# Linear attention and spectral mixing on one core: sixteen rows of one weight transfer cut into short and long transfers

## The chip, the core and the metric

The kernel runs on one core of one Trainium2 chip. A core has a matrix engine (TensorE, PE in the profile, with its weight loads listed as PEld), a vector engine (DVE), a scalar engine (ACT), a general engine (GpSimd, POOL) and a queue processor (SyncE, SP), and 16 DMA engines that move data between the chip's main memory (HBM) and the on-chip memory (SBUF, 128 partitions). POOL and SP issue the transfers; the DMA engines carry them out.

The metric is the device time of one execution in microseconds (us), as the median of three runs: 421.13 us before the change (421.12 to 421.89).

## What is computed

The reference, cut to what matters here:

```python
def _attn_ref(q, k, v):                      # (8 batches, 8 heads, 576, 64)
    q_p, k_p = phi(q), phi(k)                # elu + 1
    kv  = einsum('bhsd,bhse->bhde', k_p, v)
    num = einsum('bhsd,bhde->bhse', q_p, kv)
    den = einsum('bhsd,bhd->bhs', q_p, k_p.sum(axis=2))[..., None] + 1e-06
    return num / den                         # x: (8, 576, 512) after the heads are joined

def _moe_ref(x, w_r, w_i, w_ch):             # w_r, w_i: (64 modes, 512, 512) f32
    X = rfft(x, axis=1)
    Xr, Xi = real(X[:, :64]), imag(X[:, :64])
    Yr = einsum('bmd,mde->bme', Xr, w_r) - einsum('bmd,mde->bme', Xi, w_i)
    Yi = einsum('bmd,mde->bme', Xr, w_i) + einsum('bmd,mde->bme', Xi, w_r)
    u = x + irfft(Y, n=576, axis=1)          # Y: Yr + iYi in the first 64 modes, else 0
    return u + maximum(u @ w_ch, 0.0)
```

Nearly all the data is in `w_r` and `w_i`: 64 modes x 512 x 512 float32 each, 134 MB together. Each of these numbers is used once per execution, with 8 batches.

## The kernel before, in words

The kernel has three stages. In the first, q, k and v of the 8 batches are loaded, the attention is computed and its result is transformed to the 64 modes. In the last, the result is transformed back, added, multiplied by `w_ch` and stored. Between them, and the longest, is the stage of the modes. It takes the 64 modes in 32 pairs, `mode_pair(p)` for p from 0 to 30 and `last_pair()` for p = 31 (called `LAST`).

**What one pair needs.** Pair p needs the two matrices of modes 2p and 2p+1 from `w_r` and the two from `w_i`. `w_load(p, half, ...)` issues one transfer from POOL for `half` 0 (`w_r`) and one for `half` 1 (`w_i`). One transfer reads 64 rows of 8192 consecutive float32 numbers each and writes them, turned into bfloat16, to every second of the 128 partitions of the tile `w{p}` (`w_in[p][half::2]`, 16 blocks of 512 numbers per partition). That is 2 MB read and 1 MB written per transfer, 16 KB written per row.

**What uses it.** `mode_pair(p)` runs 16 products (`product`, line 432 of the profile) of that tile with the transformed input, into one accumulator `P`. The first of them waits until both transfers of the pair have landed. Then `evacuate` (lines 447 and 449) copies `P` out and `picks` (line 455) sorts the rows. `work_slot` fits pieces of the other stages in between (for instance lines 726, 736, 745, 751 and 752), and `keep_warm` (line 419) runs matmuls whose result is not used.

**What sets the order.** The order on every engine is written out by hand: `pin` keeps instructions in the order of the program. The pairs 5 to 31 share two buffers (`W_KEEP = 2`). So the transfers of pair p+2 are issued by POOL after the 16 products of pair p have read the buffer; POOL issues the `w_r` half, then the `w_i` half, and waits for the next buffer. Two pairs are therefore in flight or in use at any time. POOL does nothing else in this stage. Each transfer raises one of eight completion counters, taken in turn; an issue that takes a counter again waits for the counter's previous transfer.

**The last pair.** `w_load_last` (line 129) splits the last pair: `w_r` and `w_i` of mode 62, `w_r` of mode 63, and `w_i` of mode 63 in five pieces (`PIECES`: 2, 2, 2, 1 and 1 of 8 blocks). `last_pair` uses each piece as soon as it has landed (`y_last`, line 513). After the last piece the rest hangs on its result: line 519, lines 932 to 945, the exchange of rows in `YZ_all` (line 947), and the final sums and stores (lines 760 to 834).

Of the kernel before, what the change touches and what calls it, by code (L numbers as in the profile page):

```python
# [43 lines left out]
def kernel(  # L44
# [10 lines left out]
    nc = tc.nc  # L55
# [7 lines left out]
    NDW = 4 * NDC  # L63
    NDL = NDW // 2
# [41 lines left out]
    pin = tc.keep_in_program_order  # L106
    PIECES = (slice(0, 2), slice(2, 4), slice(4, 6), slice(6, 7), slice(7, 8))
    HALVES = [slice(0, 64), slice(64, 128)]

    LAST = NM // 2 - 1  # L110

    def w_load(p: int, half: int, pool, tag: str, bufs: int):
        if half == 0:
            w_in[p] = pool.tile([128, NDW, D], BF16, tag=tag, bufs=bufs, name=f"w{p}")
        two = (moe_w_r, moe_w_i)[half][2 * p : 2 * p + 2]
        pin(
            nc.gpsimd.dma_start(  # L117
                out=w_in[p][half::2], in_=two.rearrange("g (r dc) e -> (g r) dc e", dc=NDW)
            )
        )  # L120

    def w_load_last(pool, tag: str, bufs: int):
        w_in[LAST] = pool.tile([128, NDW, D], BF16, tag=tag, bufs=bufs, name=f"w{LAST}")
        for g in range(2):
            for half in range(2):
                rows_in = (moe_w_r, moe_w_i)[half][NM - 2 + g].rearrange("(p dc) e -> p dc e", dc=NDL)
                for dcs in PIECES if (g, half) == (1, 1) else (slice(0, NDL),):
                    dst = w_in[LAST][half::2, g * NDL + dcs.start : g * NDL + dcs.stop]
                    pin(nc.gpsimd.dma_start(out=dst, in_=rows_in[:, dcs, :]))
# [16 lines left out]
    def w_next():  # L146
        p, half = pending.pop(0)
        pool, tag, bufs = (wpool, "w", W_KEEP) if p < n_keep else (wpre, "wp", W_PRE)
        w_load(p, half, pool, tag, bufs)
# [258 lines left out]
    def w_get(p: int):  # L408
        if p not in w_in and p == LAST:
            w_load_last(wpool, "w", W_KEEP)  # L410
        elif p not in w_in:
            for half in range(2):
                w_load(p, half, wpool, "w", W_KEEP)
        return w_in[p]
# [14 lines left out]
    def product(P, x, n: int, w, dc: int, n_dc: int):  # L429
        c = dc % NDC * 32  # L430
        pin(
            nc.tensor.matmul(  # L432
                P[c : c + n, :], x, w[:, dc, :],
                start=(dc < NDC), stop=(dc >= n_dc - NDC), tile_position=(0, c),
                skip_group_check=True,
            )
        )

    def set_diagonal(p: int):
        for h in range(2):  # L440
            src = xt_v[HALVES[h], :, :, :, p].rearrange("p c t b -> p c (t b)")
            pin(nc.vector.tensor_copy(out=xz[p % 2][HALVES[h], :, h, :], in_=src))  # L442
# [19 lines left out]
    def mode_pair(p: int):  # L462
# [5 lines left out]
        for dc in range(NDW):  # L468
            product(P, xz[p % 2][:, dc].rearrange("p h n -> p (h n)"), 32, w, dc, NDW)
        if p + 1 < LAST:  # L470
            set_diagonal(p + 1)
# [15 lines left out]
    def last_pair():  # L487
        xl = ystage.tile([128, NDL, 2 * B], BF16, name="xl")
        for h in range(2):
            src = xt_v[:, (2 * h + 1) * NDC : (2 * h + 2) * NDC, :, :, LAST]  # L490
            pin(
# [3 lines left out]
            )  # L495
        w = w_get(LAST)
        kk = NM - 2
# [91 lines left out]
    def x_of(t: int):  # L589
        if t < B * NJJ:  # L590
            return x_main[t // NJJ][:, t % NJJ, :]
        i = t - B * NJJ
        return x_tail[i // 2][:, i % 2, :]
# [352 lines left out]
    for h, eng in enumerate((nc.sync, nc.gpsimd)):  # L946
        eng.dma_start(
            out=YZ_all[64 * h : 64 * h + 64 : NF // NL].rearrange("r b z d -> r b (z d)"),
            in_=last.rearrange("p z d -> p (z d)"),
# [15 lines left out]
    def sums_of(n: int, i: int):  # L965
# [8 lines left out]
            out=x_of(0), in0=accs[0][:, 0], scalar=0.0, in1=x_of(0), op0=ALU.max, op1=ALU.add  # L974
# [50 lines left out]
```

## Time and profile before

| | |
|---|---|
| Median of three runs | 421.13 us (421.12 to 421.89) |
| Span of the profiled execution, first to last instruction | 419.4 us |
| Median less span, what lies around the instructions | 1.7 us |
| TensorE busy | 317.2 us (76% of the span) |
| VectorE / ScalarE / GpSimd busy | 231.3 / 154.2 / 57.4 us |
| DMA engines, packets of POOL's transfers | 93.4% of the time of all 16 engines |
| One weight transfer (62 of them), median from issue to landing | 13.2 us (`w_r`), 17.5 us (`w_i`) |
| POOL's issue of one weight transfer, median | 0.544 us |
| Mean granted TensorE clock | 0.83 of full speed |

How to read it: the profile is of one execution. An engine is busy while one of its instructions runs; the DMA share is the time that packets took on the 16 DMA engines. "Issue to landing" of a transfer counts its waiting behind earlier transfers in the same queue. The trace also holds every packet of the DMA engines, with its queue, start, duration and size, and for each transfer 16 completion marks, one from each DMA engine. It doesn't say which engine a packet or mark belongs to; but each engine's packets follow each other at a fixed step, so that its packets can be followed by their times. Queue q0 holds the transfers that POOL issues, q1 those of SP; q8 and q14 are the engines' own reading of their programs.

### The profile page before, as it was taken

The page shows a single profiled execution, that of the slowest core. Times are in us where ns is not written, and L with a number is a line of the kernel's source. Part 1 is how long each engine was busy: PE and PEld are TensorE (multiplying, and loading weights), DVE is VectorE, ACT ScalarE, POOL GpSimd, SP SyncE. Part 2 cuts the span into 40 slices and gives each one's busy share as a digit, 9 for nine tenths or more (in the row PEclk, how much of TensorE's full clock was granted, in tenths as well). Part 3 has the DMA queues.
Part 4 walks back from the last instruction along what each step waited for, and adds up shares of the span by engine and source line. Part 5 has one row for each costly group of instructions (what it writes and reads, how often), then busy time and mean ns, then how long its engine had stood idle before and what let it go on. Part 6 is the DMA issues. An engine that isn't in the chain of part 4 may idle for free.

```text
span 419.4 us, 7466 instructions
## 1 busy us (share of the span) xinstructions
PE 317.2 (76%) x3143; PEld 164.4 (39%) x3143; DVE 231.3 (55%) x509; ACT 154.2 (37%) x253; POOL 57.4 (14%) x100
## 2 busy tenths in 40 slices
PE   0369998999617875676767686988798877998993
PEld 0257776877301332222222233433343332453421
DVE  4588899785314563463645353464456443522794
ACT  4677798854201011000000233334253432330783
POOL 4222224210011211111111111111111111130000
PEclk9999999579855658665655599899899997899998
DMA  8999999999999999999999999999999999998698
GB/s 217 211 212 216 210 222 203 228 206 223 217 223 208 218 220 209 220 217 212 220 214 213 223 213 214 223 210 216 220 209 219 217 214 219 216 209 166 235 391 328
DMA packets 17073, 93.17 MB, mean 222 GB/s; under 512 B 2112, under 2 KB 3024, under 8 KB 12880
## 3 DMA queue, kind: packets, MB, share of 16 engines
q0 software_dynamic: 12496, 81.48, 93.4%
q1 hardware_dynamic: 4544, 11.22, 7.2%
q8 instruction: 24, 0.39, 0.3%
q14 instruction: 9, 0.07, 0.0%
HBM read 163.93 MB, written 9.44 MB: 413 GB/s over the span
## 4 chain that ended last, share of the span: by engine, by line
DMA 64%; PE 23%; DVE 4%; POOL 3%; ACT 3%; issue 2%; DVEq 0%; ACTq 0%; POOLq 0%
DMA w<-in_moe_w_i_dram 53%; DMA pick_sb<-row_pick 8%; PE P L432 6%; DMA k<-in_k_dram 3%; PE acc L760 3%; PE kvp L257 3%; PE acc L800 2%; POOL w L117 2%; PE z L726 1%; DVE x L293 1%; ACT ke L208 1%; PE xf L355 1%; PE zl L419 1%; PE qTp L237 1%; PE num L163 1%
## 5 line engine op out<-in xcount | busy, mean ns | idle before, releaser
L432 PE MATMUL P<-w,xz 128*32 128x512 bf16 x496 | 42.6, 475 | 37.6 <-DMA w<-in_moe_w_i_dram 35.4
L419 PE MATMUL zl<-wch,id 128*128 128x512 f16 x185 | 58.2, 466 | 0.0
L449 ACT CAST ys<-P 128x512 f16<-128x512 f32 x15 | 8.8, 586 | 132.4 <-PE P L432 132.4
L117 POOL DMA_DIRECT2D w<-in_moe_w_r_dram x31 | 17.3, 559 | 246.4 <-PE P L432 211.8
L447 DVE CAST ys<-P 128x512 f16<-128x512 f32 x17 | 11.8, 692 | 51.0 <-PE P L432 51.0
L706 PE MATMUL eps<-wch,xTw 128*128 128x512 f16 x144 | 39.3, 399 | 0.0
L432 PEld LDWEIGHTS <-xz 128*32 128x32 bf16 x496 | 12.6, 108 | 63.3 <-DMA w<-in_moe_w_i_dram 40.3
L163 PEld LDWEIGHTS <-qT 64*128 64x128 f16 (+1 forms) x640 | 22.6, 122 | 29.6 <-issue 15.6
L689 ACT CAST x16w<-x_main 128x512 f16<-128x512 f32 x32 | 19.8, 618 | 37.8 <-DVE x_main L687 37.8
L687 DVE TENSOR_TENSOR x_main<-ya,x_main 128x512 f32<-128x512 f32 x32 | 22.0, 689 | 16.5 <-PE ya L683 16.3
L257 PE MATMUL kvp<-vpad,ke 32*128 32x130 f16 x576 | 24.3, 263 | 8.9 <-ACT qT L244 6.1
L442 DVE COPY xz<-xt_c 64x256 bf16<-64x256 bf16 x62 | 23.0, 371 | 10.9 <-PE P L432 10.0
L419 PEld LDWEIGHTS <-id 128*128 128x128 f16 x185 | 18.9, 112 | 25.6 <-issue 14.3
L714 ACT CAST E<-eps 128x512 f16<-128x512 f32 (+1 forms) x40 | 21.2, 540 | 17.7 <-PE eps L706 17.7
L257 PEld LDWEIGHTS <-ke 32*128 32x128 f16 x576 | 22.3, 116 | 10.6 <-issue 8.6
L163 PE MATMUL nw<-kv_sb,qT 64*128 64x65 f16 (+1 forms) x320 | 18.2, 231 | 9.8 <-DVE x_tail L650 4.7
L237 PE MATMUL qTp<-id,qe 128*128 128x128 f16 x144 | 15.1, 289 | 10.6 <-DVE qe L221 9.5
L293 DVE TENSOR_TENSOR x<-num,rd 128x512 f16<-128x512 f32 x32 | 22.1, 692 | 1.1
L650 DVE TENSOR_TENSOR x_main<-nw,rd 128x256 f32<-128x256 f32 x32 | 11.2, 416 | 18.8 <-PE nw L163 18.8
L455 PE MATMUL yt<-pick_sb,ys 128*128 128x32 f16 (+1 forms) x128 | 8.8, 185 | 16.7 <-DMA pick_sb<-row_pick 9.4
L698 DVE COPY xTw<-xTp 128x512 f16<-128x512 f16 x36 | 15.0, 416 | 10.3 <-PE xTp L696 10.3
L208 ACT ACTIVATE qe<-q 128x1152 f16<-128x1152 f16 (+1 forms) x16 | 17.9, 1157 | 7.2 <-DMA q<-in_q_dram 7.1
(118 smaller groups left out, 507.5 us busy)
## 6 DMA issues: line engine op xcount, KB each, us to landing
w<-in_moe_w_r_dram POOLq DMA_DIRECT2D x31, 1024.0 KB, 13.2
w<-in_moe_w_i_dram POOLq DMA_DIRECT2D x31, 1024.0 KB, 17.5
out_dram<-x_main SPq DMA_DIRECT2D x12, 512.0 KB, 3.6
k<-in_k_dram POOLq DMA_DIRECT2D x8, 576.0 KB, 12.9
v<-in_v_dram POOLq DMA_DIRECT2D x8, 576.0 KB, 14.3
q<-in_q_dram POOLq DMA_DIRECT2D x7, 576.0 KB, 12.6
out_dram<-x_main SPq DMA_DIRECT2D x8, 256.0 KB, 4.0
q<-in_q_dram SPq DMA_DIRECT2D x2, 576.0 KB, 4.5
```

The source lines that it names most:

```text
L117: nc.gpsimd.dma_start(out=w_in[p][half::2], in_=two.rearrange("g (r dc) e -> (g r) dc e", dc=NDW))
L163: mm = nc.tensor.matmul(num[hpo][orow, c0 : c0 + 65], qT[rows, hpp, h2, cols], kv_sb[rows, hpp, h2, :])
L208: pin(nc.scalar.activation(out=ev[:, c], in_=heads(nm, b, c), func=AF.Exp))
L257: nc.tensor.matmul(kv_ps[:, h2, 0:130], phi["k", b][r0 : r0 + 32, j // NJ, j % NJ].rearrange("p o d -> p (o d)"), vp[r0 : r0 + 32, :, j, 0 ...
L293: nc.vector.tensor_tensor(out=dst.rearrange("p (o c d) -> p o c d", o=2, c=4), in0=nv[:, :, :, 0:64], in1=rden.unsqueeze(3).broadcast_to([ ...
L419: pin(nc.tensor.matmul(last_ps[0], id16, wch16[:, 0, :]))
L432: nc.tensor.matmul(P[c : c + n, :], x, w[:, dc, :], start=(dc < NDC), stop=(dc >= n_dc - NDC), tile_position=(0, c), skip_group_check=True,)
L442: pin(nc.vector.tensor_copy(out=xz[p % 2][HALVES[h], :, h, :], in_=src))
L687: pin(nc.vector.tensor_tensor(out=x, in0=acc, in1=x, op=ALU.add))
L689: pin(nc.scalar.copy(out=x16w[t], in_=x))
L706: nc.tensor.matmul(e_ps, xT[:, c, :], wch16[:, c, :], start=(c == 0), stop=(c == NDC - 1))
L714: pin(nc.scalar.copy(out=dst, in_=e_ps[:, cols]))
```

## The change

The `w_r` transfer of pair 21 (modes 42 and 43) is issued as five transfers in place of one. Rows 0 to 47 go as one transfer of 48 rows. Rows 48 to 55 go as two transfers of 8 rows: each row's 16 blocks of 512 numbers are seen as two halves of 8 blocks; the short transfer takes the first block of each half (two runs of 512 numbers per row), the long one the other seven of each half (two runs of 3584 numbers per row). Rows 56 to 63 go the same way. The same bytes land in the same places. All other transfers are as before.

```diff
+    CUT = (21, 0)
 
     def w_load(p: int, half: int, pool, tag: str, bufs: int):
         if half == 0:
             w_in[p] = pool.tile([128, NDW, D], BF16, tag=tag, bufs=bufs, name=f"w{p}")
         two = (moe_w_r, moe_w_i)[half][2 * p : 2 * p + 2]
-        pin(
-            nc.gpsimd.dma_start(
-                out=w_in[p][half::2], in_=two.rearrange("g (r dc) e -> (g r) dc e", dc=NDW)
-            )
-        )
+        rows_in = two.rearrange("g (r dc) e -> (g r) dc e", dc=NDW)
+        if (p, half) != CUT:
+            pin(nc.gpsimd.dma_start(out=w_in[p][half::2], in_=rows_in))
+            return
+        dst = w_in[p].rearrange("p (h d) e -> p h d e", h=2)
+        src = rows_in.rearrange("p (h d) e -> p h d e", h=2)
+        pin(nc.gpsimd.dma_start(out=w_in[p][half : 2 * 48 : 2], in_=rows_in[0:48]))
+        for lo in (48, 56):
+            for d0, d1 in ((0, 1), (1, NDL)):
+                pin(
+                    nc.gpsimd.dma_start(
+                        out=dst[half + 2 * lo : 2 * lo + 16 : 2, :, d0:d1, :],
+                        in_=src[lo : lo + 8, :, d0:d1, :],
+                    )
+                )
```

Here `NDW` is 16, `NDL` is 8 and `D` is 512. In the changed program POOL issues 106 instructions instead of 102, in the same order otherwise. The first products of pair 21 wait for the five transfers of `w_r` and the one of `w_i`, and the issue for pair 23, which takes the buffer again, names these six. The later transfers keep their places relative to each other in the turn of the eight counters.

## The prediction

> **What bounds the kernel now.** I read the page's span, slices and queues first. The third number in a queue's row is the share of the 16 DMA engines' time over the span.
>
> ```profile
> span 419.4 us, 7466 instructions
> ...
> DMA  8999999999999999999999999999999999998698
> ...
> q0 software_dynamic: 12496, 81.48, 93.4%
> q1 hardware_dynamic: 4544, 11.22, 7.2%
> q8 instruction: 24, 0.39, 0.3%
> q14 instruction: 9, 0.07, 0.0%
> ```
>
> The DMA engines are full from the first slice to slice 37 (about 388 us). TensorE is busy too, but much of that is filler, so I read next the chain of work that ended last, around pair 21 and at the end of the loads (start, length, what):
>
> ```profile
> 253.72 17.46 DMA w<-in_moe_w_i_dram
> 271.18 0.04 issue
> 271.22 1.07 PE P L432 x16
> 272.29 0.29 issue
> 272.58 0.54 POOL w L117
> 273.12 17.50 DMA w<-in_moe_w_i_dram
> 290.62 0.04 issue
> ...
> 369.52 1.01 PE P L432 x16
> 370.52 0.29 issue
> 370.81 2.16 POOL w L129 x4
> 372.98 13.65 DMA w<-in_moe_w_i_dram
> 386.63 0.05 issue
> 386.67 0.36 PE y_last L513 x8
> ```
>
> A pair's products start 0.04 us after its `w_i` half has landed, and `y_last` 0.05 us after a piece of the last pair. So the end follows the last landings. The issue at 272.58 is pair 21's. Its long wait is not a gap: the queue still holds pair 20. Landings of whole transfers follow each other every 4.85 us from 130 to 375 us, whatever the issues do. What sets the time is the DMA engine that finishes last.
>
> That is the third view, the DMA share in 40 slices from 380 to 388 us (0.2 us each):
>
> ```profile
> DMA  9599599569889989999899334666566555454100
> ```
>
> It falls from 9 to 3 at 384.4 us and ends only at 387.6. So the 16 engines do not finish together. Following their packets (each 16 KB packet takes 1227 ns and the next starts 1208 ns after it) I find the ends: six engines at 384.20 to 384.42, one at 384.73, two at 386.45 and 386.60, seven at 387.34 to 387.62. At 23 us all 16 landing marks of a transfer lay within 0.34 us.
>
> The cause is in q8 and q14, the reading of programs. A q8 packet is 16 KB, and 23 of the 24 come before 388 us. Their durations repeat in a cycle of eight (975, 975, 962, 893, 893, 948, 945, 935 ns): eight engines take turns. From 140 us on, the engine hit loses 858 to 940 ns. That makes three hits for seven engines and two for the eighth (hit at 219.0, end at 386.60). The q14 packets (8 KB, 322 ns) hit two others in turn, 300 ns each time. These end at 384.73 and 386.45. Thus eight **program-reading engines** are late (seven of them by 3 us), and of the other eight one is late by 2.1 us.
>
> **The change, part by part.** All is worked against the profiled execution: 419.4 us of span, 1.7 us less than the median of 421.13.
>
> *Rows 0 to 47.* 48 rows over 16 engines are 3 packets instead of 4: each engine saves 1208 ns.
>
> *Four transfers of 8 rows.* Each has 16 packets: 1 KB written in the short, 7 KB in the long. Rows of q0: 1 KB takes 98 ns, 2 KB 173, 8 KB 625, 16 KB 1227; less the overlap of 19 ns the steps are 79, 154, 606 and 1208 ns. A 7 KB packet lies between 2 and 8 KB; on their line it is 531 ns. Completion marks add about 21 ns per transfer and engine (a weight transfer takes 4853 ns, four steps are 4832): 84 ns for four.
>
> The trace of before has no transfer of 8 rows, so which engines take these packets is open. Per engine, against the 4853 ns before:
> - the short ones on eight engines, two packets each: -1208 + 4 x 79 + 84 = **-0.81 us** for those;
> - the long ones on the other eight: -1208 + 4 x 531 + 84 = **+1.00 us** for those;
> - both kinds on the same eight: -1208 + 4 x 610 + 84 = +1.32 us there, -1.12 on the others;
> - spread evenly over 16: -1208 + 2 x 610 + 84 = +0.10 us everywhere.
>
> Below nothing the bound is -1.12 us, above it +1.32. I take short and long on opposite eights, since the two kinds are separate transfers that each fill eight engines with two packets.
>
> The Trainium skill speaks to this on the page "DMA: Bandwidth & Descriptors", section "Why a DMA increments its semaphore by 16 and not by 1": a software-issued transfer over fewer than 16 engines goes to consecutive engines from a cursor that goes round. By that rule the short ones meet on one eight and the long ones on the other; no run here shows it yet.
>
> *What counts of this.* The delay of an engine stays with it to the end, since its queue never runs dry: the fetch delays above did. So the landing that ends the loads moves by the sum on the latest engine. There are two answers for opposite eights. If any of the seven latest engines gets long packets, the end moves from 387.62 to between 387.34 + 1.00 = 388.34 and 388.62: **+0.7 to +1.0 us**. If all eight program-reading engines get the short ones, they end at 386.8, but the engine at 386.45 goes to 387.45, which is then last: 387.45 - 387.62 = **-0.2 us**.
>
> *Issue on POOL.* Four more issues at 0.544 us (rows of L117) are 2.18 us: the `w_i` half of pair 21 is issued from 275.30 instead of 273.12. Nothing else queues behind it on POOL until 282.34. The earliest engine needs it only at 282.43, the first landing mark of pair 21's `w_r`; the exchange near the end, into an idle queue, took 2.0 us from POOL's issue (390.49) to its first packet (392.47). Issued by 275.85, it is ready at 277.8, with 4.6 us of cover (3.8 on an engine that saves 0.81 us). Price nothing; without the cover it would be at most 2.18 us. The first short pieces are covered as well: the first issue still ends at 273.12, and pair 20 keeps even the earliest engine until 277.58.
>
> *Waits.* The products of pair 21 wait for six transfers instead of two; the `w_i` half lands last by 4.85 us, so the five others are done. The issue for pair 23 names six transfers that have landed before the products it also waits for. SP has no transfers of its own in this stretch. Nothing.
>
> *Cost per transfer.* The pieces of the last pair measure it: 128 KB pieces land 0.63 to 0.64 us apart, 64 KB ones 0.32 to 0.34, against 0.61 and 0.30 for their share of a whole transfer: 0.02 to 0.04 us each, packets included. This is in the sums. The page named above, section "Anatomy of one DMA", gives about 2.0 us fixed per such transfer. By it four more in line would cost 8 us and end at 429 us; the rows above say that the queue hides that part.
>
> *After the loads.* If the landings come 1.0 us later, pair 29's `w_i` lands at 369.3, still before its products at 369.52; pair 30's products (378.10, on a landing at 378.05) and `y_last` follow the landing. POOL's last issue at 378.34 moves to 379.3 and is ready at 381.3, before the earliest engine comes to it (384.2, or 383.4 with short packets). All later work hangs on line 519 and shifts whole.
>
> Sum for the likeliest case: at least one of the seven latest engines in the long eight, likely one of the last ones: +0.7 to +1.0, I take +0.97. Span 420.4, median **422.1 us**.
>
> **The rivals.**
> *A, no slower: the short packets fall on exactly the eight program-reading engines.* -0.2 us, 420.95 us. For it: these eight are a closed group, and the two q14 engines lie outside it, as if engines were given out in halves. Against it: nothing shows that the group is a run of eight, or that the short transfers start on it. The point of decision: all seven of the latest engines must be spared; one in the long eight is enough for +0.7. Even then the gain cannot reach 0.2%: the engine at 386.45 takes back 0.63 of the 0.81 us.
> *B, all four on the same eight engines.* +1.32 (422.45 us) if one of the seven is there; otherwise the engine at 386.45 ends at 387.77, +0.15 (421.3 us). For it: 8 rows may be handed out from the same first engine each time. Against it: nothing in the trace.
> *C, spread evenly, so the change moves nothing.* +0.10 us, 421.2 us. For it: every other transfer here loads all 16 engines alike. Against it: 8 rows don't divide by 16.
> *D, the cover fails:* the issues arrive late and the late engines run dry. At most +2.2 us. The 3.8 us of cover speak against it.
>
> **How the numbers follow.** About 0.2% (0.84 us) is what a measurement of this kernel can tell from no change. The likeliest case has 0.50, A 0.30, B 0.10 in two equal halves, C 0.06, D 0.02, and 0.02 is left for a gain that I don't see. Of the likeliest case about nine tenths lie above 0.84 us, since five of the seven latest engines end within 0.16 us of the last. Slower: 0.45 + 0.05 + 0.02, and some more because the unknown extras add, 0.54; faster 0.03; same the rest, 0.43. The range reaches from A's 420.9 to B's 422.5; the likeliest case's own range is 421.8 to 422.3.
>
> **What would show it.** In the profile after: 66 weight issues from POOL, five of them from 272.58 on at 0.54 us steps; before that everything unchanged. The packets of 1 KB and 7 KB show as 98 and about 550 ns. If the likeliest case is right, the spread of the engines' ends grows from 3.4 us to 4 or more, a landing and `y_last` come about 1 us later, and the chain between line 519 and the end is as long as now. If A is right the late group ends near 386.8 and the spread shrinks to about 2.3 us. If B, some engines of the same transfer are 2.4 us apart. I am wrong if pairs 22 to 31 show new idle time on POOL or TensorE, if a delay is caught up before the end, or if the small packets take much longer than their rows.

## The result and the profile after

The changed kernel takes 422.47 us (median of 11 runs, 422.11 to 422.74) against 421.21 us for the kernel before on the same chip (11 runs). The ratio is 1.0024, with a 95% interval of 1.0016 to 1.0032: slower by 1.26 us by the medians. In a second measurement it was 422.58 against 421.25 us, ratio 1.0030 (1.0018 to 1.0042). The profiled execution has a span of 420.8 us against 419.4.

Line numbers after the change are higher by 11 from `w_load_last` on (L432 is L443, L519 is L530). The ordinary weight transfer is L119, the 48-row transfer L123, the four small ones L127.

From the page of the changed kernel, the span, the DMA slices and POOL's queue:

```profile
span 420.8 us, 7473 instructions
...
DMA  8999999999999999999999999999999999997698
...
q0 software_dynamic: 12672, 81.48, 93.2%
```

The same bytes move in 176 more packets, and the DMA engines are as full as before. The other queues have the same packets and bytes. The three steps of the prediction are read one after the other below.

First the issue. The timeline of POOL in the changed kernel (start, length, what, and in brackets the idle time before it):

```profile
272.55 0.52 POOL L123 DMA_DIRECT2D w<-in_moe_w_r_dram  x1 [7.72 <-PE P L443]
273.09 2.27 POOL L127 DMA_DIRECT2D w<-in_moe_w_r_dram  x4
275.36 0.57 POOL L119 DMA_DIRECT2D w<-in_moe_w_i_dram  x1
282.45 0.57 POOL L119 DMA_DIRECT2D w<-in_moe_w_r_dram  x1 [6.52 <-PE P L443]
```

Four issues of about 0.57 us were added where POOL would have been idle, and the next issue, at 282.45 us, is not pushed by them.

Second the landings. From the chain of work that ended last, around pair 21 and at the end of the loads:

```profile
264.28 16.76 DMA w<-in_moe_w_i_dram
281.04 0.04 issue
281.09 1.08 PE P L443 x16
282.16 0.29 issue
282.45 0.56 POOL w L119
283.01 18.24 DMA w<-in_moe_w_i_dram
...
361.43 17.47 DMA w<-in_moe_w_i_dram
378.90 0.04 issue
378.94 1.08 PE P L443 x16
380.02 0.02 issue
380.04 0.70 DVE ys L458
380.75 0.04 issue
380.79 0.27 PE yt L466 x4
381.06 3.85 PE zl L430 x10
...
389.46 0.20 PE y_last L524 x8
389.66 0.02 issue
389.68 0.23 DVE Y L530
```

Pair 30's `w_i` lands at 378.90 us, where it landed at 378.05 before. The last landing of all comes at 388.81 against 387.88: +0.93 us. In the kernel before the chain's end reads:

```profile
387.85 0.36 PE y_last L513 x8
388.20 0.02 issue
388.23 0.24 DVE Y L519
```

In the packets, 1 KB takes 96 to 98 ns and 7 KB 548 or 549 ns. The 16 landing marks of pair 21's `w_i` half spread over 5.03 us, where those of a weight transfer in the kernel before spread over at most 3.4.

Third, what the chain does after 380.79 is new. It does not go back to a landing but through ten filler matmuls that take 3.85 us. The same group in the timelines of TensorE, first of the changed kernel, then of the kernel before:

```profile
380.91 4.00 PE L430 MATMUL zl<-wch,id 128*128 128x512 f16 x10
```

```profile
380.06 2.32 PE L419 MATMUL zl<-wch,id 128*128 128x512 f16 x10
```

The reason is in the windows of the changed kernel. The columns are the window, its length, busy time and count of TensorE, of its weight loads, VectorE, ScalarE and POOL, then the granted TensorE clock, the DMA share and GB/s:

```profile
380.00:382.00 2.00, 1.21 (x7) 0.51 (x8) 1.03 (x3) 0.00 (x0) 0.00 (x0) 0.75 0.97 200
382.00:384.00 2.00, 2.00 (x6) 0.73 (x5) 0.00 (x0) 0.00 (x0) 0.00 (x0) 0.50 1.04 204
384.00:386.00 2.00, 2.00 (x11) 0.66 (x13) 0.00 (x0) 0.00 (x0) 0.00 (x0) 0.90 0.73 138
```

From 381.0 to 384.4 us the granted clock was half. In the kernel before it was 1.00 in all three windows, and its half-clock stretch lay at 351.9 to 358.7:

```profile
380.00:382.00 2.00, 2.00 (x14) 0.94 (x15) 0.25 (x2) 0.00 (x0) 0.00 (x0) 1.00 0.98 203
382.00:384.00 2.00, 2.00 (x15) 0.63 (x14) 0.00 (x0) 0.00 (x0) 0.00 (x0) 1.00 1.02 199
384.00:386.00 2.00, 1.90 (x11) 0.46 (x9) 1.32 (x2) 0.00 (x0) 0.00 (x0) 1.00 0.66 122
```

So the cast of Y (L530) starts 0.88 us after the last landing, against 0.34 us before. In this one execution the cast is 1.45 us later (389.68 against 388.23): about 0.93 of it from the landings, about 0.54 from TensorE. From that cast to the end of VectorE's last sum it is 25.86 us, against 25.88: nothing was gained or lost there.

### The profile page after: what moved, and what is told of

It reads as the page before. It is cut to its first block, busy times and chain, and to the rows that moved or that the text cites. A ratio compares the mean times of both kernels' runs of the same rounds, so it can differ in the third digit from the quotient of the medians.

```text
span 420.8 us, 7473 instructions
## 1 busy us (share of the span) xinstructions
PE 321.5 (76%) x3143; PEld 164.9 (39%) x3143; DVE 230.8 (55%) x509; ACT 153.9 (37%) x253; POOL 59.6 (14%) x104
## 4 chain that ended last, share of the span: by engine, by line
DMA 62%; PE 23%; DVE 6%; issue 3%; ACT 2%; POOL 2%; DVEq 0%; POOLq 0%; ACTq 0%
DMA w<-in_moe_w_i_dram 49%; DMA pick_sb<-row_pick 8%; PE P L443 6%; DMA k<-in_k_dram 5%; PE zl L430 3%; PE acc L771 3%; PE acc L811 2%; PE kvp L268 2%; POOL w L119 2%; PE eps L717 1%; ACT ke L219 1%; DVE x L304 1%; PE z L737 1%; DVE ke L232 1%; PE xf L366 1%
## 5 line engine op out<-in xcount | busy, mean ns | idle before, releaser
L443 PE MATMUL P<-w,xz 128*32 128x512 bf16 x496 | 46.8, 515 | 34.0 <-DMA w<-in_moe_w_i_dram 31.6
L430 PE MATMUL zl<-wch,id 128*128 128x512 f16 x185 | 60.7, 482 | 0.0
L119 POOL DMA_DIRECT2D w<-in_moe_w_r_dram x30 | 16.8, 559 | 236.1 <-PE P L443 217.6
L717 PE MATMUL eps<-wch,xTw 128*128 128x512 f16 x144 | 40.6, 409 | 0.0
L443 PEld LDWEIGHTS <-xz 128*32 128x32 bf16 x496 | 13.3, 113 | 61.4 <-DMA w<-in_moe_w_i_dram 36.4
L466 PE MATMUL yt<-pick_sb,ys 128*128 128x32 f16 (+1 forms) x128 | 8.7, 184 | 17.5 <-DMA pick_sb<-row_pick 10.2
L248 PE MATMUL qTp<-id,qe 128*128 128x128 f16 x144 | 13.3, 265 | 11.2 <-DVE qe L232 9.5
L174 PE MATMUL num<-kv_sb,qT 64*128 64x65 f16 (+1 forms) x320 | 16.6, 219 | 5.0 <-DVE x L304 2.1
```

The lines of the kernel that those rows point to most:

```text
L119: pin(nc.gpsimd.dma_start(out=w_in[p][half::2], in_=rows_in))
L174: mm = nc.tensor.matmul(num[hpo][orow, c0 : c0 + 65], qT[rows, hpp, h2, cols], kv_sb[rows, hpp, h2, :])
L430: pin(nc.tensor.matmul(last_ps[0], id16, wch16[:, 0, :]))
L443: nc.tensor.matmul(P[c : c + n, :], x, w[:, dc, :], start=(dc < NDC), stop=(dc >= n_dc - NDC), tile_position=(0, c), skip_group_check=True,)
L717: nc.tensor.matmul(e_ps, xT[:, c, :], wch16[:, c, :], start=(c == 0), stop=(c == NDC - 1))
```

## The experiments

The theory behind the prediction, T: a transfer of eight rows reaches eight of the 16 DMA engines, the short and the long ones reach opposite eights, and the engines that are latest anyway and get the long packets end 1.0 us later. The rival R: the four more transfers cost time by themselves. Unless said otherwise a diff is against the changed kernel, and a difference in us is between medians on the same chip.

**The order of the second pair turned round.** Short, long, long, short instead of short, long, short, long: the same transfers and bytes, issued in as many steps.

```diff
+    PARTS_CUT = ((48, 56, 0, 1), (48, 56, 1, 8), (56, 64, 1, 8), (56, 64, 0, 1))
...
-        for lo in (48, 56):
-            for d0, d1 in ((0, 1), (1, NDL)):
...
+        for lo, hi, d0, d1 in PARTS_CUT:
```

> The five transfers of the change, but the second group of 8 rows goes long first, then short. Theory T (unequal shares): the short and long transfers of 8 rows fall on alternate eights of the DMA engines, so now every engine gets two packets of 1 KB and two of 7 KB: -1.208 + 2 x 0.079 + 2 x 0.531 + 0.084 = +0.10 us on each, no change that can be measured (about +0.1 us), and the engines' ends at the end of the loads as far apart as in the kernel before (3.4 us). Rival R (the small transfers themselves: more issues, marks, waits): the same five transfers and the same packets as the change, so about +1.0 to +1.3 us as the change.

Measured: 421.71 us against 421.52, ratio 1.0007 (0.9998 to 1.0016), no measurable change. The chain of this kernel at the end:

```profile
387.90 0.32 PE y_last L524 x8
388.23 0.02 issue
388.25 0.23 DVE Y L530
```

Its last landing is at 387.91 us, as in the kernel before (387.88), and the marks spread 3.33 us. (The profiled execution is the fastest of its eleven, 421.42 us.) T holds and R falls: five transfers in place of one cost nothing that can be measured, if each engine gets one short and one long pair. The interval leaves them at most 0.16%, or 0.67 us in all. The Trainium skill's figure of about 2.0 us fixed for such a transfer ("DMA: Bandwidth & Descriptors", section "Anatomy of one DMA") does not show in the time here: an estimate from it for four in line would be 8 us. What the same page says in "Why a DMA increments its semaphore by 16 and not by 1", that transfers over fewer than 16 engines go on from a cursor that goes round, is what makes the order matter; the result agrees with it.

**The short packets turned by six and by ten places.** By T the group of short packets can be moved by putting first a transfer of 6 or 2 rows. In the changed kernel's trace six of the eight program-reading engines get long packets and two get short ones; so if the eight stand in a row, one of the two positions must spare them.

```diff
+    PARTS_CUT = ((48, 54, 1, 8), (48, 56, 0, 1), (56, 64, 1, 8), (56, 64, 0, 1), (54, 56, 1, 8))
```

```diff
+    PARTS_CUT = ((48, 50, 0, 1), (48, 56, 1, 8), (56, 64, 0, 1), (56, 64, 1, 8), (50, 56, 0, 1))
```

> The same bytes cut in another order and at one more place: long of 6 rows, short of 8, long of 8, short of 8, long of 2, so that by theory T the short packets fall on the 7th to 14th engine of the turn and the long ones on the other eight. In the changed kernel's trace six of the eight engines that carry program reads get long packets and two get short ones, so the group of eight begins two engines before or after an eight of the turn. If it begins at the 7th, all eight get the short packets (-0.79 us) and the last to end is the engine with the small program reads, 386.45 + 1.02 = 387.47 against 387.62: -0.15 us, no measurable change. If it begins at the 11th, four of the seven latest engines get long packets: +1.0 us. Rival R (small transfers cost by themselves): +1.0 us or more here and in the kernel with the other shift.

> The mirror image: short of 2 rows, long of 8, short of 8, long of 8, short of 6, so that by theory T the short packets fall on the 11th to 16th and the 1st and 2nd engine of the turn. If the group of program-reading engines begins at the 11th: -0.15 us, no measurable change; if it begins at the 7th: +1.0 us. Theory T says that exactly one of the two shifted kernels is slow if the group is a run of eight; if both are slow by about 1 us it is no run of eight, or the rival R holds.

Measured: 422.52 us, ratio 1.0022 (1.0013 to 1.0030), and 422.71 us, ratio 1.0023 (1.0013 to 1.0034), both against 421.52. The last landings are at 389.06 and 389.22 us. Both are as slow as the change itself, and R has fallen with the mirrored order. So the latest engines are not eight in a row. Where they are had to be seen.

**Which engine is which.** Rows 48 to 63 were cut two at a time, each group with a short size of its own (1 to 7 KB), so that a packet's size tells its place in the turn. In a second kernel the first group had three rows, which shifts all others by one.

```diff
+    PARTS_CUT = ((48, 50, 0, 1), (50, 52, 0, 2), (52, 54, 0, 3), (54, 56, 0, 4), (56, 58, 0, 5), (58, 60, 0, 6), (60, 62, 0, 7), (62, 64, 0, 8), (48, 50, 1, 8), (50, 52, 2, 8), (52, 54, 3, 8), (54, 56, 4, 8), (56, 58, 5, 8), (58, 60, 6, 8), (60, 62, 7, 8))
```

```diff
+    PARTS_CUT = ((48, 51, 0, 1), (51, 53, 0, 2), (53, 55, 0, 3), (55, 57, 0, 4), (57, 59, 0, 5), (59, 61, 0, 6), (61, 63, 0, 7), (63, 64, 0, 8), (48, 51, 1, 8), (51, 53, 2, 8), (53, 55, 3, 8), (55, 57, 4, 8), (57, 59, 5, 8), (59, 61, 6, 8), (61, 63, 7, 8))
```

> One look, to see which engines of the turn carry the program reads. Rows 48 to 63 go two rows at a time: the first seven pairs of rows each as a first transfer of 1, 2, ... 7 KB runs and a later one of the rest, the eighth pair whole. By theory T each transfer of 2 rows falls on the next two engines of the turn, so the packet size tells the place in the turn, and the time at which an engine starts its packets tells how late it is. From the kernels run so far T expects two late engines among places 1 to 8, one of them at 7 or 8, five among 9 to 14 and one at 15 or 16. Each engine gets 16 KB in all, as before; but the transfers are 15, more than the eight counters, so issues wait for landings and the time is some us longer (+2 to +8 us). If T is wrong and small transfers do not go round the engines, the same size will appear on engines of any number.

> The same look shifted by one place: a first group of 3 rows, then pairs, so that pairs of engines are split otherwise. Together with the other look it gives single engines. T expects the same late engines as the other look; time again some us longer (+2 to +8 us), since issues wait for landings.

Measured, one run each: 429.49 and 428.93 us against 421.25. These times are those of another bottleneck. From POOL's timeline in the first of the two:

```profile
273.08 2.82 POOL L127 DMA_DIRECT2D w<-in_moe_w_r_dram  x5
276.25 0.55 POOL L127 DMA_DIRECT2D w<-in_moe_w_r_dram  x1 [0.34 <-DMA w<-in_moe_w_r_dram]
281.28 0.55 POOL L127 DMA_DIRECT2D w<-in_moe_w_r_dram  x1 [4.48 <-DMA w<-in_moe_w_i_dram]
284.80 4.40 POOL L127 DMA_DIRECT2D w<-in_moe_w_r_dram  x8 [2.97 <-DMA w<-in_moe_w_r_dram]
```

With 16 transfers in one half POOL waits up to 4.48 us for landings before it issues the next. By the semaphores named in the issues, eight completion counters are used in turn, and a transfer waits until the one eight before it has landed. The change itself, with five, stays below that.

The arrivals answer the question. In the first kernel the 4 KB packets go to the places 6 and 7, counted from 0 where the 8-row transfers of pair 21 start: one of these engines starts them at 280.95 us, the other at 283.00. In the second they go one place on, to 7 and 8, and start at 280.74 and 280.91. So 7 and 8 are early and 6 is late. Read so for all sizes, and together with the two turned kernels' traces: the program-reading engines, which are late by about 2 to 3 us, are at places **5, 6, 9, 10, 11, 12, 13 and one of 14 and 15**. The engine at place 3 is late by 1.3 to 1.8 us at this point; it fits the one that ended at 386.45 us in the kernel before. The other seven are early. In an eight-and-eight cut, places that lie eight apart always get opposite kinds, and 5 and 13 are both late. So no such cut can spare the latest engines, wherever it starts, and the two turned kernels are slow for that reason: one has long packets on 5 and on the late one of 14 and 15, the other on 5, 6 and 9.

**The cut on two pairs.** Pairs 12 and 21.

```diff
-    CUT = (21, 0)
+    CUT = ((12, 0), (21, 0))
...
-        if (p, half) != CUT:
+        if (p, half) not in CUT:
```

> The change applied to pair 12 as well as to pair 21. Theory T (a delay of an engine stays with it to the end of the loads, since its queue never runs dry): twice the shift, the engines with the long packets lose 2.0 us in all, so +1.8 to +2.0 us and landings at the end about 1.9 us later than in the kernel before. If late engines catch up while the early ones wait for new issues, it is less: the +0.9 to +1.3 us of the change, or near it.

Measured: 423.30 us, +2.05, ratio 1.0051 (1.0039 to 1.0064). Delays of the latest engines add, and one from pair 12 stays to the end. The profiled execution is the slowest of the five (424.10 us). From its chain:

```profile
376.66 13.10 DMA w<-in_moe_w_i_dram
389.76 0.05 issue
389.81 0.36 PE y_last L524 x8
390.16 0.23 PE zl L430
390.40 0.29 PE y_last L524 x8
390.69 0.02 issue
390.71 0.24 DVE Y L530
```

Here the chain is back on a landing, and the cast starts 0.34 us after the last one (390.37), as before the change.

**The change once more.** The same kernel, for a second profile.

> The changed kernel once more, on another chip perhaps. Theory T: again +0.9 to +1.3 us, the last landing about 388.8 us. If the half-clock stretch on the filler matmuls of the last pairs is a matter of chance, this profile need not have it, and line 530 then comes about 0.35 us after the last landing.

Measured: 422.58 us, +1.33, as given above. In this execution no half clock fell on the last fillers, and the cast starts 0.34 us after the last landing. So the 0.54 us of the first profile are not part of what the change always costs. But the last landing is at 389.24, +1.36 us, more than the packets' sum of +1.0. This surplus is what the remaining runs are about.

**Fewer fillers ahead of the last pair's products**, to take TensorE out of the way, in the changed kernel and in the kernel before:

```diff
-    FILL = {**{p: 7 for p in range(5, 16)}, **{p: 7 for p in range(18, 27)}, 27: 7, 28: 10, 29: 12, 30: 10}
+    FILL = {**{p: 7 for p in range(5, 16)}, **{p: 7 for p in range(18, 27)}, 27: 7, 28: 10, 29: 12, 30: 3}
```

> The changed kernel with 3 instead of 10 filler matmuls behind pair 30 (their results are not used). In the profiled run of the changed kernel a stretch of half clock from 381.0 to 384.4 us made these ten take 4.0 us instead of 2.3, and line 530 came 0.87 us after the last landing, where it was 0.35 us in the kernel before. Theory T: the landings alone give +0.93 us; the rest of the +1.26 us comes from TensorE reaching the last pieces late in some executions. Then this kernel is at +0.9 to +1.0 us with less spread. If the filler has nothing to do with it, it stays at +1.2 to +1.3 us.

> The kernel before with three filler matmuls instead of ten ahead of the last pair's products; the output stays the same. The same edit on the changed kernel gave 423.0 us, +1.7 to +1.8 us against the kernel before, where +0.9 to +1.0 was expected, and its half-clock stretch lay in the tail. If the fewer fillers themselves bring the half clock there (the throttle's stretch comes after the idle time that they leave), this kernel too is slower by 0.7 to 1.3 us than the kernel before (421.9 to 422.6), with a tail of 26.6 to 27.2 us behind the cast of Y instead of 25.88. If the place of that stretch was chance or belongs to the later landings, it stays within 0.3 us of the kernel before.

Measured: the changed kernel 423.00 us against 421.52, ratio 1.0037 (1.0024 to 1.0050), a miss. The kernel before 421.61 against 421.60, ratio 1.0009 (1.0000 to 1.0018), with a last landing at 388.01. In the profile of the first, from the windows (columns as above):

```profile
389.00:394.00 5.00, 4.88 (x29) 2.68 (x28) 1.78 (x4) 2.00 (x5) 0.56 (x1) 0.66 0.04 10
394.00:400.00 6.00, 6.00 (x29) 2.15 (x29) 5.23 (x9) 4.84 (x10) 0.00 (x0) 1.00 0.99 334
```

A half-clock stretch (389.7 to 393.1 us) fell into the work behind the loads: from the cast of Y to VectorE's last sum it took 27.13 us instead of 25.87. This profile is of the slowest of five runs (423.80). The kernel before, with as few fillers, keeps its 25.86 in the profile, and its median does not move. But that profile is of a run at 421.58 us, and four of its eleven runs took 422.30 to 422.96, while none of the 17 runs of the kernel before on that chip took over 421.87. So it is not shown whether fewer fillers bring such a stretch in some executions; what decides its place stays open.

**The cut on pair 30 instead of pair 21.**

```diff
-    CUT = (21, 0)
+    CUT = (30, 0)
```

> The same cut, on the w_i half of pair 30 instead of pair 21; nothing else moves. What is to be told apart: the packet sum puts the last landing +1.0 us late, while the changed kernel's medians are +1.26 and +1.33 us, and its traces show between 290 and 375 us single 16 KB packets of 1.3 to 3.2 us that no program read explains (the kernel before and the mirrored kernel have none). Theory V: the surplus over the sum comes from those packets, in pairs 22 to 30, where the early engines, now further ahead of the latest one, run out of work before a late issue. Cut at pair 30 there are no such pairs left: no such packet between 290 and 375 us, last landing 388.8 to 388.95, time +0.9 to +1.05 us (422.2 to 422.3 on a base of 421.25). Theory W: the surplus belongs to the small transfers themselves, wherever they stand: last landing 389.1 to 389.3 and +1.25 to +1.4 us. If the cut at pair 30 gave nothing at all (below +0.4), the delay would need many pairs to reach the end, against the packet sum.

(The half that is cut is `w_r`, as in the change; the expectation names the wrong one.) Measured: 423.41 us against 421.60, ratio 1.0042 (1.0027 to 1.0056). The six runs fall into two groups, three at 422.59 to 422.64 and three at 424.18 to 424.26; the median lies between them, and no run took it. The profiled execution is of the lower: last landing 389.08 us, +1.20. A delay put in only 25 us before the end counts in full; that it needs many pairs is out. On the surplus both theories missed: V wanted no slow packets, and there are ten that no program read explains between 290 and 375 us; W wanted 389.1 to 389.3, and one group of runs is near +1.0, the other at +2.6. From POOL's timeline:

```profile
362.71 0.52 POOL L123 DMA_DIRECT2D w<-in_moe_w_r_dram  x1 [10.47 <-PE P L443]
363.25 2.27 POOL L127 DMA_DIRECT2D w<-in_moe_w_r_dram  x4
365.52 0.57 POOL L119 DMA_DIRECT2D w<-in_moe_w_i_dram  x1
```

The kernel before issues that half at 361.59:

```profile
361.59 0.54 POOL L117 DMA_DIRECT2D w<-in_moe_w_r_dram  x1 [10.24 <-PE P L432]
```

The 48-row transfer itself was late here, since a half-clock stretch (353.7 to 360.5, where the kernel before has it at 351.9 to 358.7) held up the products that it waits for. The slow packets begin at 364.5, before any small packet has come. So they follow a late issue, and no small packet is needed for them. The upper group of runs has no profile, and its +2.6 us stays unexplained.

**A late issue without the cut, and an early one with it.** The fillers behind pair 27 lie ahead of the products on which the issue for pair 30 waits. Ten more in the kernel before, six fewer in the changed one:

```diff
-    FILL = {**{p: 7 for p in range(5, 16)}, **{p: 7 for p in range(18, 27)}, 27: 7, 28: 10, 29: 12, 30: 10}
+    FILL = {**{p: 7 for p in range(5, 16)}, **{p: 7 for p in range(18, 27)}, 27: 17, 28: 10, 29: 12, 30: 10}
```

```diff
-    FILL = {**{p: 7 for p in range(5, 16)}, **{p: 7 for p in range(18, 27)}, 27: 7, 28: 10, 29: 12, 30: 10}
+    FILL = {**{p: 7 for p in range(5, 16)}, **{p: 7 for p in range(18, 27)}, 27: 1, 28: 10, 29: 12, 30: 10}
```

> The kernel before with ten more filler matmuls (17 instead of 7) behind pair 27's work, so that TensorE comes to the products of pair 28 some 2.3 us later and POOL issues pair 30's first half at about 363.9 instead of 361.6 us; the output stays the same. No transfer is cut. In the profile of the kernel before, the earliest engines finish what they hold at about 365 us, and an issue takes about 2 us to reach them. Theory V: the single slow 16 KB packets of the changed kernel come from such late issues, and the latest engines lose 0.2 to 0.3 us with them. Then this kernel shows, at 364 to 369 us, packets of over 1.3 us that no program read explains (the kernel before has none), and the last landing comes at 388.1 to 388.4 instead of 387.88; time +0.2 to +0.5 us. Theory W: slow packets belong to the cut transfers and to what they leave behind; then there are none here, the last landing stays at 387.9 and the time within 0.2 us.

> The changed kernel with one filler matmul instead of seven behind pair 27's work, so that pair 30's first half is issued as soon as pair 28's products have followed their landing, at about 360.9 us; the output stays the same. Theory V: with the late issue gone no early engine runs dry at 365 us, the last landing comes at the packet sum, 388.8 to 388.95, and the time is +0.9 to +1.1 us instead of +1.26 to +1.33. Theory W: nothing changes, slow packets near 365 us remain, last landing 389.1 to 389.3, time +1.25 to +1.4 us.

Measured, with the late issue and no cut: 422.14 us against 421.49, ratio 1.0021 (1.0009 to 1.0033), with runs from 421.30 to 423.30. The profiled one, 423.15 us, is of a group of four at 423.15 to 423.30; the other five took 421.30 to 422.14. Its timelines of TensorE and of POOL:

```profile
358.93 4.52 PE L419 MATMUL zl<-wch,id 128*128 128x512 f16 x17
363.39 1.05 PE L432 MATMUL P<-w,xz 128*32 128x512 bf16 x16
```

```profile
364.75 0.54 POOL L117 DMA_DIRECT2D w<-in_moe_w_r_dram  x1 [12.63 <-PE P L432]
365.29 0.55 POOL L117 DMA_DIRECT2D w<-in_moe_w_i_dram  x1
```

The issue came at 364.75 us, later than meant, because part of the fillers ran at half clock. At 366.0 to 367.0 there are ten slow 16 KB packets of 1.36 to 2.57 us, in a kernel with no small transfer but those of its last pair; the kernel before has none. The packets therefore come with late issues, without any cut. The late transfer's marks run from 371.56 to 373.15 us, where they run from 369.78 to 373.12 in the kernel before: the early engines lost up to 1.8 us, the latest ones nothing. The last landing came at 388.72, +0.84 us, more than the 0.2 to 0.5 expected. This arises one transfer later, on a single engine: its mark comes at 378.91, the next one at 378.05, which is the last in the kernel before; and a program read of 0.94 us starts at 376.86. In this profile TensorE's own work reached the end last. The size of the effect can't be carried over to the change from this run.

With the cut and the early issue: 422.62 us against 421.49, +1.13, ratio 1.0032 (1.0022 to 1.0042). The last landing is at 388.84 us, where V wanted it, and nine slow packets remain, against 35 in the second profile of the change. The issue still came at 362.34 instead of 360.9, since the products themselves ran into a half clock (1.90 instead of 1.05 us); that is later than in the kernel before (361.59), so the run did not make the issue early. The time lies between the two theories, and its interval covers both: as a test of the time it is inconclusive.

All profiles side by side, from the traces. "Slow packets" are 16 KB packets over 1235 ns from 120 us to 385 us that no program read explains; "half clock" is the stretches after 339 us and before the last work. Each row's landing, packets and half clock are of one execution, its median of all runs.

| kernel | medians, us | last landing | cast after landing | slow packets | half clock |
|---|---|---|---|---|---|
| before | 421.13 (three runs) | 387.88 | 0.34 | 0 | 351.9 for 6.8 |
| mirrored | +0.19 | 387.91 | 0.34 | 1 | 352.8 for 6.8 |
| before, fewer fillers | +0.01 | 388.01 | 0.34 | 0 | 352.8 for 6.8 |
| before, late issue | +0.65 | 388.72 | 1.27 | 10 | 339.8 for 3.4, 353.5 for 6.8 |
| changed | +1.26 | 388.81 | 0.88 | 16 | 340.0 and 381.0 for 3.4 |
| changed, early issue | +1.13 | 388.84 | 0.34 | 9 | 352.2 for 10.2 |
| short turned by six | +1.00 | 389.06 | 0.34 | 11 | 341.0 for 3.4, 354.6 for 6.8 |
| cut on pair 30 | +1.81 (two groups) | 389.08 | 0.34 | 16 | 340.0 for 3.4, 353.7 for 6.8 |
| changed, fewer fillers | +1.48 | 389.10 | 0.34 | 12 | 389.7 for 3.4 |
| short turned by ten | +1.19 | 389.22 | 0.34 | 12 | 352.6 for 10.2 |
| changed, again | +1.33 | 389.24 | 0.34 | 35 | 341.3 for 3.4, 354.9 for 6.8 |
| cut on two pairs | +2.05 | 390.37 | 0.34 | 71 | 342.5 for 3.4, 356.2 for 6.8 |

Three balanced or uncut kernels land at 387.88 to 388.01. All that put long packets on latest engines once land 0.9 to 1.4 us later. The packets' sum (+0.99) is about the floor of that; what lies above it, 0 to 0.4 us, comes with slow packets, though not in step with their number.

## Why the prediction was right, and where it was not

The time lies within the range, close to its upper end; the likeliest case came about with a larger size: 422.47 us where 422.1 was given, by medians +1.26 and +1.33 where +0.97 was given. The likeliest case's own range, 421.8 to 422.3, was missed. That the whole range still held the time is luck: it went up to 422.5 for rival B, which did not happen, and not for what made the time longer.

- *Which engines get what.* Right: short and long on opposite eights. The prediction had no row of its own for this, only the reason that the transfers are separate and the skill's rule. The mirrored kernel shows it by taking the loss away, and the spread of 5.03 us at pair 21 shows the engines drawn apart. Rivals B and C fall with that: with both kinds on the same eight the mirrored order would have changed nothing, and an even spread could not widen the marks.
- *The packets.* The 7 KB packet took 548.5 ns, less 19 ns of overlap a step of 529.5 against the 531 used. -1208 + 4 x 529.5 + 84 gives +0.99 us. The landing moved by 0.93, 0.96 and up to 1.36 us in the profiles of the change and its variants.
- *Rival A.* It was given 0.30 because the eight program-reading engines might be a run of eight. They are not. Places 5 and 13 alone exclude it, and with them every cut into two eights. The engine at 386.45, which bounds the gain in A, is one that the small program reads hit by the prediction; these reads take 0.3 us each, and seven of them go to two engines before 388 us, so they explain at most 1.2 of its 2.1 us. Where the rest comes from is open.
- *The issue on POOL.* Right for pair 21: four more issues ran beside idle time, and cost nothing in the mirrored kernel. Rival D did not happen there.
- *Waits, cost per transfer.* Right: nothing, within the 0.67 us that the mirrored kernel leaves.
- *The tail.* Right: 25.86 against 25.88 us from the cast of Y to VectorE's last sum.
- *What failed* is the step "After the loads", and with it the sentence that a queue never runs dry. The latest engines do keep their delay, but the early ones lose part of their lead: behind the cut the marks of a transfer spread by 5.0 us, at the end by 4.4 in the first profile of the change; in the second it is 5.4 and 3.0. The sum took the landing for the whole move, with all else shifting whole. Two things came on top. The latest engine's delay holds up the products and so POOL's issues for later pairs, while the short packets let other engines run ahead. The cover of each later issue, the time by which it is ready before an engine needs it, shrinks from both ends, and with TensorE at half clock it is used up: in the second profile of the change the issue for pair 30 comes at 363.61 us instead of 361.59, engines stand idle for 0.6 us until 364.9, and packets take up to 3.23 us. That packets slow down behind a late issue is shown by the late issue without a cut; why they do is not. That they are the whole surplus is not: in the second profile seven engines, program-reading ones among them, each lose 0.19 to 0.27 us on one packet at 367.5 to 368.3 us, which fits, but the early-issue kernel did not bring the time down by a measurable amount. The other thing is where the half clock falls. It cost 0.54 us in the first profile of the change, and nothing in the second.

So the mechanism was right, and the term that was mis-sized is the move of the end after the landing: 0.97 us predicted, 1.0 to 1.33 measured in five measurements of the change and its turned and early-issue variants. No version faster than the kernel before came out of this: even with all the program-reading engines spared, the engine at 386.45 us would leave at most 1.2 us between it and the present last one, before it is given any of the rows taken from them. That estimate, under 0.3%, was not tried.

## What to carry to other kernels

In a kernel whose end is set by the last of 16 DMA engines, ask of any reshaped transfer how many bytes each engine gets, not how many in all: of two orders of the same five transfers, one cost 1.26 us and the other nothing that could be measured. Here transfers of fewer rows than engines went on from where the one before stopped, so pair a light one and a heavy one such that the turn comes round to the opposite kind (short, long, long, short). And when one engine becomes later, check the cover of the issues that wait for it, over all the stages behind the edit and at the lower clock too.

## What the runs showed of the hardware that was not expected

- The program reads of 16 KB (about 0.9 us each) go to eight fixed engines in turn, at places 5, 6, 9 to 13 and 14 or 15 (from 0, as the 8-row transfers of pair 21 count them), three to an engine in most cases before the loads end. That is most of the 3.4 us by which the engines of the kernel before end apart. Small reads of 0.3 us go to two other engines, one of them probably at place 3.
- Single 16 KB packets, 1226 to 1227 ns otherwise, took up to 3.23 us shortly after a late issue. In the changed kernel's first profile six of them lie at 247.7 to 250.2 us, before the cut; no uncut kernel with its issues in time had any.
- The half-clock stretches of TensorE, multiples of 3.4 us, lie at another place in nearly every kernel here. In one kernel such a stretch cost 1.26 us behind the loads, in another 0.54 ahead of the last products, in most nothing. What sets their place remains open.
